# Token stage of a hash-attention and MLP-mixer kernel: the second token weight's sums first on VectorE, the channel weight's sums as two jobs, a fourth place for the last part

## The chip, the cores and the metric

One core of one Trainium2 chip runs the whole kernel. The metric is the device time in microseconds (us) of that core; the kernel before takes 766.55 us, the median of 3 runs (766.54 to 766.57).

## The reference, cut to what matters

```python
# attention: B, H, S, D = 4, 8, 768, 64; only keys in the query's hash bucket count
scores = where(mask, scale * q @ k.T, -1e9); attn = softmax(scores)
x = (attn @ v) as (B, S, H * D)                  # (4, 768, 512)
# token mixing, w_tok1 (768, 256), w_tok2 (256, 768)
xt = x.transpose(0, 2, 1)
h = np.maximum(xt @ w_tok1, 0.0) @ w_tok2
u = x + h.transpose(0, 2, 1)
# channel mixing, w_ch1 (512, 1536), w_ch2 (1536, 512)
h2 = np.maximum(u @ w_ch1, 0.0) @ w_ch2
return u + h2
```

## The kernel before, in words

The program has three stages that follow one another: attention (function `attention`), token mixing (`tokens`), channel mixing (`channels`). Each engine works through its own list of instructions in order; semaphores hold an instruction until what it needs is there. The order of the lists is the order in which the code is written, and the memory of a tile that is given back may be taken by a later tile, whose first write then waits for everything that used the old one.

**The activations.** `XT` in SBUF holds x, later u, transposed: 128 partitions by 4 column blocks by 4 x 768 rows. A copy of x lies in DRAM (`bounced`), from which `tokens` fetches the rows of batch element b into `x0` (b even) or `x1` (b odd).

**The token stage** goes over b = 0 to 3. `mix1(b)` makes the hidden layer in two halves j (24 matmul instructions each, L1226), and ScalarE applies the ReLU after each half (L1233). `left_sums(b)` makes four sums on VectorE (L1249 to L1252). `mix2(b, m)`, m = 0 and 1, makes two column blocks of the second product with seven half-size products in place of eight (L1266), for which it needs sums of the weight `W2`: `weight_sums()` inside `tokens` (L1203 to L1206). Its results go from four PSUM banks by four ScalarE copies (L1271, L1274, L1276, L1278) and five VectorE adds (L1281 to L1285) into a *place* in SBUF, and from there GpSimd's queue starts a transfer that adds the place to `XT` (L1286). There are three places, the three thirds of the later tile `SW2`; part (b, m) takes place (2b + m + 1) mod 3, so part (3,1) takes the place that (2,0) took, and its first copy must wait until the transfer of (2,0) has read it. The eight transfers of GpSimd's queue signal the semaphores DMASW0 to DMASW7 in turn, part (3,1) the last.

**The jobs.** Between the parts, work for the channel stage is done as a list of jobs: one after each half of `mix1`, one between the two parts of `mix2` of b = 0, 1, 2: eleven turns. The first job makes the sums of the channel weight `WC1` (four VectorE operations of 128 x 1536, L1316 to L1321: `early` the first two, `late` the other two), the other eight convert pieces of the second channel weight from 64-bit floats: one operation on ScalarE (L177), then five on VectorE (L187 to L206), 768 columns each.

**The channel stage** begins with the pass `hidden(0, t)`, t = 0 to 5, called row t here. Each row is seven products of 1.72 us (L1353) into four banks, in two pairs of banks; the pairs alternate between two rows. The products 1 to 4 fill the four banks; ScalarE copies three of them (L1359: p1 from the first bank, p5, p7); products 5 to 7 go on adding to banks 1, 3 and 4, each behind the copy of its bank; then a VectorE add makes the first result `R[0]` (L1393), and ScalarE makes a fourth copy, u, of the first bank. Three more adds (L1402) and a bounded difference (L1368) end the row. Between them VectorE makes sums of weights for later (L1858 to L1861 for each part, L1316 to L1321 once more for the second channel weight, on tiles that include the three places), which SyncE's queue stores in DRAM. GpSimd adds two copies per row (L1397). `R[0]` lies in memory that `x0` had.

Of the kernel before, what the change touches and what calls it, by code (L numbers as in the profile page):

```python
# [48 lines left out]
def kernel(  # L49
# [18 lines left out]
    B, NP, _, _, S = qk.shape  # L68
# [1116 lines left out]
    def tokens(pool, psum, W1, W2, x0, weights, jobs, T, places):  # L1185

        x1 = pool.tile([P, NR, DM], F32, name="x1", tag="x1", bufs=1)
        R1 = {}
        turned = not jobs
        if not turned:
            fetch(1, x1)
            jobs = jobs(weights(pool))
            bounce(places[2], NREG - 2)
        NQ = DM // 2
        sums = pool.tile([P, 3, HALF], F32, name="W2sums", tag="W2sums", bufs=1)
        b00, b01, b10, b11 = (W2[:, k, HALF * n : HALF * n + HALF] for k in range(2) for n in range(2))  # L1200

        def weight_sums():
            nc.vector.tensor_tensor(sums[:, 0], b01, b00, op=ALU.subtract)  # L1203
            nc.vector.tensor_tensor(sums[:, 1], b11, sums[:, 0], op=ALU.subtract)
            nc.vector.tensor_tensor(b01, b11, b01, op=ALU.subtract)
            nc.vector.tensor_tensor(sums[:, 2], b10, sums[:, 1], op=ALU.subtract)  # L1206

        def job():
            if not turned and jobs:
                jobs.pop(0)()  # L1210

        def bank(name):
            return psum.tile([P, 512], F32, name=name, tag="mm", bufs=4 if turned else 8)

        def banks():
            return psum.tile([P, 2, 512], F32, name="trp", tag="tr", bufs=2)

        def mix1(b):
            x = (x0, x1)[b % 2]
            if b and turned:  # L1220
                turn(b, x, banks)
            r1 = pool.tile([P, NJ, DM], F32, name="r1", tag="r1", bufs=2)
            for j in range(NJ):
                ps = bank("t1")
                for r in range(NR):
                    nc.tensor.matmul(  # L1226
                        ps, W1[:, r, P * j : P * j + P], x[:, r], start=(r == 0), stop=(r == NR - 1),
                    )
                to = r1[:, j]
                if not turned:  # L1230
                    to = to.rearrange("p (c g i) -> p g c i", c=NCB, i=32)
                    ps = ps.rearrange("p (g c i) -> p g c i", c=NCB, i=32)
                nc.scalar.activation(to, ps, ACT.Relu)  # L1233
                job()
            if b % 2:
                new = pool.tile([P, 3, NQ], F32, name="r1s", tag="r1s", bufs=1)
            else:
                new = T[0].rearrange("p k t -> p (k t)")[:, : 3 * NQ].rearrange("p (i c) -> p i c", i=3)
            R1[b] = r1, new
            if not turned and b + 2 < B:  # L1240
                fetch(b + 2, x)

        def left_sums(b):
            r1, new = R1[b]
            a00, a01, a10, a11 = (
                r1[:, k].rearrange("p (m i c) -> p i m c", m=2, i=2)[:, i] for i in range(2) for k in range(2)
            )
            new = new.rearrange("p i (m c) -> p i m c", m=2)
            nc.vector.tensor_tensor(new[:, 1], a00, a10, op=ALU.subtract)  # L1249
            nc.vector.tensor_tensor(a10, a10, a11, op=ALU.add)  # L1250
            nc.vector.tensor_tensor(new[:, 0], a10, a00, op=ALU.subtract)
            nc.vector.tensor_tensor(new[:, 2], a01, new[:, 0], op=ALU.subtract)  # L1252

        def mix2(b, m):

            r1, new = R1[b]
            a00, a01, s1, a11 = (
                r1[:, k, P * (2 * m + i) : P * (2 * m + i) + P] for i in range(2) for k in range(2)
            )
            new = new[:, :, P * m : P * m + P]  # L1260
            ps = [bank("t2")[:, :HALF] for _ in range(4)]
            to = places[(2 * b + m + 1) % 3].rearrange("p (i n t) -> p i n t", i=2, n=2)
            p1, u, p7, p57 = (to[:, i, n] for i in range(2) for n in range(2))

            def product(at, left, right, start=True):
                nc.tensor.matmul(  # L1266
                    ps[at], left, right, start=start, stop=True, skip_group_check=True,
                )

            product(0, a00, b00)  # L1270
            nc.scalar.copy(p1, ps[0])  # L1271
            product(1, a01, b10)
            product(2, s1, sums[:, 0])
            nc.scalar.copy(p57, ps[2])  # L1274
            product(3, new[:, 1], b01)
            nc.scalar.copy(p7, ps[3])  # L1276
            product(0, new[:, 0], sums[:, 1], False)
            nc.scalar.copy(u, ps[0])  # L1278
            product(2, new[:, 2], b11, False)
            product(3, a11, sums[:, 2], False)  # L1280
            nc.vector.tensor_tensor(p1, ps[1], p1, op=ALU.add)  # L1281
            nc.vector.tensor_tensor(p57, p7, p57, op=ALU.add)
            nc.vector.tensor_tensor(p57, p57, u, op=ALU.add)
            nc.vector.tensor_tensor(p7, ps[3], u, op=ALU.add)
            nc.vector.tensor_tensor(u, ps[2], u, op=ALU.add)  # L1285
            nc.gpsimd.dma_start(  # L1286
                out=XT[:, 2 * m : 2 * m + 2, S * b : S * b + S], in_=to.rearrange("p i n t -> p i (n t)"),
                accum_op=ALU.add,
            )

        for b in range(B):
            mix1(b)
            if b == 0:
                weight_sums()
            left_sums(b)
            if b:
                mix2(b - 1, 0)
                job()
                mix2(b - 1, 1)
        mix2(B - 1, 0)  # L1300
        inputs(0, T, 0)
        mix2(B - 1, 1)
        while not turned and jobs:
            job()

    def weight_sums(w, sums, first, second, low, high):

        a00, a01 = w[:, first, low], w[:, second, low]
        a10, a11 = w[:, first, high], w[:, second, high]

        def early():
            nc.vector.tensor_tensor(sums[:, 1], a00, a10, op=ALU.subtract)  # L1316
            nc.vector.tensor_tensor(a10, a10, a11, op=ALU.add)

        def late():
            nc.vector.tensor_tensor(sums[:, 0], a10, a00, op=ALU.subtract)  # L1320
            nc.vector.tensor_tensor(sums[:, 2], a01, sums[:, 0], op=ALU.subtract)  # L1321

        return [early, late]
# [892 lines left out]
    def inside(stage, *args):  # L2216
        with tc.tile_pool(name="sb", bufs=2, reuse_waits="tile") as pool, tc.tile_pool(
            name="ps", bufs=2, space=PSUM, reuse_waits="tile"
        ) as psum, tc.manual_schedule():
            stage(pool, psum, *args)  # L2220
# [8 lines left out]
    late = ctx.enter_context(ExitStack())  # L2229
    big = {}  # L2230
    n = NHT // 4 * P
# [10 lines left out]
    def attention_and_tokens(W1, W2, x0):  # L2242
        inside(attention, W1, W2, x0)
        pool = late.enter_context(tc.tile_pool(name="late", bufs=1, side="right", reuse_waits="tile"))
        SW1 = big["SW1"] = pool.tile([P, 3, NCB // 2, DCH // 2], F32, name="SW1")
        TA = big["TA"] = pool.tile([P, 2, NCB // 2, TT], F32, name="TA")
        n = NHT * DM

        def second_tile(i):
            return pool.tile([P, (n, n * 3 // 4)[i]], F32, name=f"second{i}", tag=f"second{i}", bufs=1)  # L2250

        WC2 = second["WC2"] = second_tile(0).rearrange("p (k c) -> p k c", k=NHT)
        second["SW2"] = second_tile(1).rearrange("p (i k c) -> p i k c", i=3, k=NHT // 2)
        second["tile"] = second_tile

        def weights(pool):
            return Conversion(pool, [(w_ch2, WC2, 3, (0, NHT))], bufs=3)

        def jobs(conversion):
            early, late = weight_sums(  # L2260
                WC1, SW1, slice(0, NCB // 2), slice(NCB // 2, NCB), slice(0, DCH // 2), slice(DCH // 2, DCH),
            )
            return [
                lambda: (early(), late()),
                *[conversion.one] * (NHT * DM // NW),
            ]

        SW2 = second["SW2"].rearrange("p i k c -> p i (k c)")
        places = [SW2[:, i] for i in range(3)]
        inside(tokens, W1, W2, x0, weights, jobs, [TA[:, 0], None, TA[:, 1], None], places)  # L2270
# [100 lines left out]
```

## Time and profile before

| what | value |
|---|---|
| median of 3 runs | 766.55 us |
| the profiled execution's own time | 767.96 us |
| its span, first to last instruction | 766.2 us |
| TensorE busy (PE) | 758.5 us, 99% of the span |
| VectorE busy (DVE) | 673.5 us, 88% |
| ScalarE busy (ACT) | 442.4 us, 58% |
| token stage, first matmul of `mix1(0)` to the first of row 0 | 289.12 to 367.64 us |
| first channel pass, rows 0 to 5 | 367.64 to 439.74 us |

Durations and starts are read from one profiled execution, in us from the start of its span. A line of the timeline gives the start, the duration, the engine, the line of the kernel, the operation, output<-input, the shape, and in brackets how long the engine stood idle before it and what released it. PEld is TensorE's loading of weights, which runs beside its matmuls; POOL is GpSimd, SP is SyncE's queue of transfers. The 1.76 us by which the execution's time is longer than its span lie outside the instructions.

### The profile page before, as it was taken

To read this page: it belongs to the slowest core of one execution; us is meant where nothing else is said; L and a number is where in the kernel's file an instruction comes from. 1 tells how busy PE (TensorE), PEld (TensorE's weight loads), DVE (VectorE), ACT (ScalarE), POOL (GpSimd) and SP (SyncE) were. 2 spreads that over 40 slices of the span, in tenths; PEclk is the share of its full clock that TensorE was granted. 3 is DMA by queue.
4 is the path that set the end of the run, shared out by engine and by line. 5 is a ranking of instruction groups with operands and counts; after the bars stand their busy time and mean duration, and the time that the engine had idled before them with its cause. 6 is when DMAs were issued, how large, how long until landed. Compare 5 with 4: busy or idle time off the path is not lost.

```text
span 766.2 us, 14575 instructions
## 1 busy us (share of the span) xinstructions
PE 758.5 (99%) x5549; PEld 509.8 (67%) x5549; DVE 673.5 (88%) x969; ACT 442.4 (58%) x816; POOL 189.7 (25%) x266
## 2 busy tenths in 40 slices
PE   9999999999999999999999999999999999999997
PEld 4565655666656554455444468888877888886886
DVE  5899899899997998999788798998899799889884
ACT  6677777677776873333232326566666667665331
POOL 2346771638761820011220100100000011000001
PEclk9999999999999999999999999999999999999999
DMA  7746587575965549876697997889576696750665
GB/s 257 271 172 184 179 240 225 181 179 186 217 202 116 168 68 254 310 178 119 112 321 244 348 360 263 244 233 277 171 220 210 234 261 140 235 157 8 207 157 130
DMA packets 131210, 157.80 MB, mean 206 GB/s; under 512 B 56000, under 2 KB 99520, under 8 KB 129216
## 3 DMA queue, kind: packets, MB, share of 16 engines
q1 hardware_dynamic: 119248, 136.05, 56.3%
q0 software_dynamic: 11600, 20.53, 13.1%
q8 instruction: 45, 0.74, 0.4%
q10 hardware_dynamic: 288, 0.25, 0.1%
q14 instruction: 29, 0.24, 0.1%
HBM read 107.71 MB, written 40.67 MB: 194 GB/s over the span
## 4 chain that ended last, share of the span: by engine, by line
PE 88%; DVE 8%; DMA 2%; issue 1%; SPq 0%; DVEq 0%; ACT 0%; ACTq 0%
PE b L1353 51%; PE sc L503 16%; PE acc L470 14%; PE sc L425 1%; PE hash L536 1%; PE ss L848 1%; DVE size L196 1%; PE sacc L874 1%; DVE unit L195 1%; DMA XT<-second 1%; DVE second L206 1%; PE hash L348 1%; DVE size L191 1%; PE ssums L862 1%; PE hash L353 1%
## 5 line engine op out<-in xcount | busy, mean ns | idle before, releaser
L414 ACT ACTIVATE exps<-sc 128x768 f32<-128x768 f32 (+1 forms) x181 | 126.5, 765 | 10.1 <-PE sc L503 7.2
L1353 PE MATMUL b<-R,second 128*128 128x256 f32 (+1 forms) x522 | 131.8, 408 | 0.0
L503 PE MATMUL sc<-qk 32*128 32x384 f32 (+1 forms) x1352 | 120.1, 457 | 0.0
L1353 PEld LDWEIGHTS b<-R,second 128*128 128x128 f32 x522 | 99.1, 190 | 28.5 <-issue 16.5
L470 PE MATMUL acc<-exps,vn 128*32 128x385 f32 (+1 forms) x1344 | 111.7, 486 | 0.0
L503 PEld LDWEIGHTS sc<-qk 32*128 32x128 f32 x1352 | 92.3, 185 | 16.9 <-issue 4.4
L1359 ACT COPY c<-b 128x256 f32<-128x256 f32 (+1 forms) x96 | 40.3, 426 | 79.3 <-PE b L1353 66.1
L470 PEld LDWEIGHTS acc<-exps,vn 128*32 128x32 f32 x1344 | 43.9, 109 | 62.0 <-issue 60.0
L376 POOL DMA_DIRECT2D bits<-XT x104 | 54.6, 526 | 72.1 <-DVE XT L366 27.4
L459 DVE TENSOR_TENSOR esd<-esd,exps 128x768 f32<-128x768 f32 x70 | 67.0, 957 | 4.3
L1353 PE MATMUL b<-XT,WC 128*128 128x256 f32 (+1 forms) x208 | 61.0, 428 | 0.0
L791 POOL DMA_INDIRECT table<-XT,sorting x48 | 57.1, 1190 | 14.7 <-issue 13.2
L2063 POOL DMA_DIRECT2D out<-second x7 | 8.5, 1213 | 187.3 <-DVE second L2057 81.5
L557 ACT COPY rec<-rec 32x384 f32<-32x384 f32 x56 | 28.5, 510 | 41.0 <-DVE rec L551 39.6
L1353 PEld LDWEIGHTS b<-XT,WC 128*128 128x128 f32 x208 | 39.5, 190 | 15.4 <-issue 10.3
L503 PE MATMUL sc<-bits 32*128 32x384 bf16 (+1 forms) x338 | 48.0, 311 | 0.0
L1353 PE MATMUL b<-XT,SW 128*128 128x256 f32 (+1 forms) x164 | 47.0, 410 | 0.0
L455 DVE TENSOR_TENSOR esd<-esd,exps 128x768 f32<-128x768 f32 x42 | 40.3, 958 | 4.4
L1226 PE MATMUL t<-x,W 128*128 128x512 f32 x96 | 42.1, 594 | 0.2 <-DMA x<-bounced 0.2
L1353 PEld LDWEIGHTS b<-XT,SW 128*128 128x128 f32 x164 | 31.1, 190 | 9.4 <-issue 4.1
L1286 POOL DMA_DIRECT2D XT<-second x8 | 9.9, 1233 | 95.8 <-DVE unit L187 56.2
L1226 PEld LDWEIGHTS t<-x,W 128*128 128x128 f32 x96 | 18.1, 190 | 23.3 <-issue 21.7
(333 smaller groups left out, 1455.9 us busy)
## 6 DMA issues: line engine op xcount, KB each, us to landing
second<-left SPq DMA_DIRECT2D x20, 768.0 KB
qk<-in_qk_rows SPq DMA_DIRECT2D x13, 1152.0 KB
raw<-in_moe_w_ch SPq DMA_DIRECT2D x16, 768.0 KB
second<-left SPq DMA_DIRECT2D x18, 576.0 KB
WC<-hidden_left SPq DMA_DIRECT2D x18, 448.0 KB
x<-bounced SPq DMA_DIRECT2D x4, 1536.0 KB
XT<-second POOLq DMA_DIRECT2D x8, 768.0 KB
seen<-in_qk SPq DMA_DIRECT2D x15, 384.0 KB
```

What stands on the lines that cost most here:

```text
L376: nc.gpsimd.dma_start(out=to[at : at + 2 * BITS, half[j]], in_=g[of : of + 2 * BITS])
L414: return nc.scalar.activation(e[:, :, columns], sc, ACT.Exp, scale=SCALE)
L455: nc.vector.tensor_tensor(self.d, self.d, e, op=ALU.add)
L459: nc.vector.tensor_tensor(self.d, self.d, e, op=ALU.add)
L470: made = nc.tensor.matmul(acc[D * i + d : D * i + d + 32], vn[:, i, c, d : d + 32], e[:, i], start=(c == 0), stop=(c == NR - 1),)
L503: nc.tensor.matmul(made[j, piece][:, i], k[at : at + 32, ks], q[at : at + 32], start=part < 0, stop=part == 1,)
L557: nc.scalar.copy(rec[other : other + 32, h], rec[at : at + 32, h])
L791: nc.gpsimd.indirect_dma_start(out=tables[2 * w + i], out_offset=bass.IndirectOffsetOnAxis(ap=self.at[:, x : x + 1], axis=0), in_=row, in_ ...
L1226: nc.tensor.matmul(ps, W1[:, r, P * j : P * j + P], x[:, r], start=(r == 0), stop=(r == NR - 1),)
L1286: nc.gpsimd.dma_start(out=XT[:, 2 * m : 2 * m + 2, S * b : S * b + S], in_=to.rearrange("p i n t -> p i (n t)"), accum_op=ALU.add,)
L1353: nc.tensor.matmul(ps, left(k), right(k), start=start and k == ks[0], stop=stop and k == ks[-1], skip_group_check=True,)
L1359: nc.scalar.copy(c, ps)
```

## The change

Three edits, all in the token stage:

1. `weight_sums()` of `tokens` is called ahead of the loop over b, no longer after `mix1(0)`.
2. The sums of the channel weight, one job with four VectorE operations, become two jobs with two each. There are now ten jobs in the same eleven turns, so each conversion comes one turn later.
3. Part (3,1) of `mix2`, the last, puts its results into the memory of `x0`, in place of the place that (2,0) used. `x0` holds batch element 2 before, which `mix1(2)` has read.

```diff
-            to = places[(2 * b + m + 1) % 3].rearrange("p (i n t) -> p i n t", i=2, n=2)
+            place = places[(2 * b + m + 1) % 3]
+            if b + 1 == B and m:
+                place = x0.rearrange("p r c -> p (r c)")[:, : 2 * S]
+            to = place.rearrange("p (i n t) -> p i n t", i=2, n=2)
...
+        weight_sums()
         for b in range(B):
             mix1(b)
-            if b == 0:
-                weight_sums()
             left_sums(b)
...
             return [
-                lambda: (early(), late()),
+                early, late,
                 *[conversion.one] * (NHT * DM // NW),
             ]
```

In the changed kernel the lines behind the first edit are numbered 3 higher, those behind the second 2 higher (L1271 becomes L1274, L1393 becomes L1395).

The list of VectorE at the start of the token stage, before. `SW` and `WC` are the channel weight and its sums, `W` is `W2`, `W2sums` its sums, the rows of `unit`, `size` and `second` one conversion:

```order
L1316 TENSOR_TENSOR SW_3789<-WC_85 128x1536
L1317 TENSOR_TENSOR WC_85<-WC_85 128x2x768
L1320 TENSOR_TENSOR SW_3789<-WC_85 128x1536
L1321 TENSOR_TENSOR SW_3789<-WC_85,SW_3789 128x1536
L187 TENSOR_SCALAR unit<-size 128x768
L191 TENSOR_SCALAR size<-size 128x768
L195 SCALAR_TENSOR_TENSOR unit<-raw,unit 128x768
L196 TENSOR_TENSOR size<-size,unit 128x768
L206 SCALAR_TENSOR_TENSOR second_3791<-raw,size 128x3x256
L1203 TENSOR_TENSOR W2sums<-W_109 128x384
L1204 TENSOR_TENSOR W2sums<-W_109,W2sums 128x384
L1205 TENSOR_TENSOR W_109<-W_109 128x384
```

The same place in the changed kernel; the last four rows are `left_sums(0)`:

```order
L1203 TENSOR_TENSOR W2sums<-W_109 128x384
L1204 TENSOR_TENSOR W2sums<-W_109,W2sums 128x384
L1205 TENSOR_TENSOR W_109<-W_109 128x384
L1206 TENSOR_TENSOR W2sums<-W_109,W2sums 128x384
L1318 TENSOR_TENSOR SW_3789<-WC_85 128x1536
L1319 TENSOR_TENSOR WC_85<-WC_85 128x2x768
L1322 TENSOR_TENSOR SW_3789<-WC_85 128x1536
L1323 TENSOR_TENSOR SW_3789<-WC_85,SW_3789 128x1536
L1249 TENSOR_TENSOR TA<-r_3818 128x256
L1250 TENSOR_TENSOR r_3818<-r_3818 128x2x128
L1251 TENSOR_TENSOR TA<-r_3818 128x256
L1252 TENSOR_TENSOR TA<-r_3818,TA 128x256
```

One conversion has moved from ahead of `left_sums(0)` to behind it; from there on, up to `mix2(1,1)`, each step of VectorE has one conversion fewer ahead of it.

The list of ScalarE at `mix1(3)` and the start of `mix2(2,0)`, before:

```order
L1233 ACTIVATE r_4040<-t_4041 128x4x4x32
L177 ACTIVATE size<-raw 128x768
L1233 ACTIVATE r_4040<-t_4057 128x4x4x32
L1271 COPY second_3792<-t_4070 128x384
L1274 COPY second_3792<-t_4072 128x384
L1276 COPY second_3792<-t_4073 128x384
```

And in the changed kernel:

```order
L1233 ACTIVATE r_4032<-t_4033 128x4x4x32
L177 ACTIVATE size<-raw 128x768
L1233 ACTIVATE r_4032<-t_4049 128x4x4x32
L177 ACTIVATE size<-raw 128x768
L1274 COPY second_3792<-t_4070 128x384
L1277 COPY second_3792<-t_4072 128x384
```

The last conversion now begins behind the ReLU of the second half of `mix1(3)`, where it began behind the first half.

The list of VectorE where the token stage ends and row 0 begins, with the semaphores that each row waits for, before:

```order
L1284 TENSOR_TENSOR second_3792<-t_4138,second_3792 128x384 [waits PE_49]
L1181 TENSOR_TENSOR TB<-XT,TA 128x1024
L1285 TENSOR_TENSOR second_3792<-t_4137,second_3792 128x384 [waits DVE_49]
L1183 TENSOR_TENSOR TB<-XT,TB 128x1024 [waits DVE_49]
L1393 TENSOR_TENSOR R_4169<-b_4176,c 128x2x256 [waits DMAHW5_49,PE_49,Activation_49]
L1394 TENSOR_SCALAR R_4169<-R_4169 128x2x256 [waits DVE_49]
```

And in the changed kernel, where `x` is `x0`:

```order
L1287 TENSOR_TENSOR x_110<-t_4138,x_110 128x384 [waits PE_49]
L1288 TENSOR_TENSOR x_110<-t_4137,x_110 128x384 [waits DVE_49]
L1181 TENSOR_TENSOR TB<-XT,TA 128x1024
L1183 TENSOR_TENSOR TB<-XT,TB 128x1024 [waits DVE_49]
L1395 TENSOR_TENSOR R_4169<-b_4176,c 128x2x256 [waits DMASW7_49,PE_49,Activation_49]
L1396 TENSOR_SCALAR R_4169<-R_4169 128x2x256 [waits DVE_49]
```

The first write of `R[0]` waited for the transfer that had fetched batch element 2 into `x0` (DMAHW5); it now waits for DMASW7, the transfer of part (3,1), which reads its place in `x0`.

## The prediction

> **What bounds the kernel now.** First the table of windows: one line per `mix2` part of interest, then the first channel pass and the rest.
>
> ```profile
> core 0: us, PE busy (x) PEld busy (x) DVE busy (x) ACT busy (x) POOL busy (x), PEclk, DMA share, GB/s
> 310.31:314.82 4.51, 4.51 (x15) 2.61 (x14) 4.34 (x9) 3.20 (x6) 0.00 (x0) 1.00 1.04 401
> 314.82:319.60 4.78, 4.78 (x16) 2.58 (x15) 4.64 (x7) 2.54 (x5) 0.00 (x0) 1.00 0.48 157
> 362.77:367.64 4.87, 4.78 (x15) 2.58 (x14) 4.53 (x7) 1.72 (x4) 1.22 (x1) 1.00 0.50 89
> 367.64:439.74 72.10, 72.10 (x169) 31.90 (x168) 56.48 (x85) 18.71 (x34) 11.43 (x8) 1.00 0.85 265
> ```
>
> TensorE sets the end: in the first channel pass it is busy for 72.10 of 72.10 us, at a granted clock of 1.00, so what it loses at any point from here on is lost at the end. In the token stage an undisturbed part takes 4.51 us; part (0,1) takes 4.78 and part (3,1) 4.87. These 0.27 + 0.36 = 0.63 us are all that the three edits can take away there. The timeline shows what held the two parts:
>
> ```profile
> 316.21 0.93 ACT L177 ACTIVATE size<-raw 128x768 f32<-128x768 f32 x1 [2.00 <-DVE second L206]
> 317.03 0.47 ACT L1271 COPY second<-t 128x384 f32<-128x384 f32 x1
> 317.56 0.30 PEld L1266 LDWEIGHTS t<-W2sums,TA 128*128 128x128 f32 x2 [0.61 <-ACT second L1271]
> ...
> 358.57 1.20 POOL L1286 DMA_DIRECT2D XT<-second  x1 [6.89 <-DVE second L1285]
> 365.07 0.48 ACT L1271 COPY second<-t 128x384 f32<-128x384 f32 x1 [2.91 <-DMA XT<-second]
> 365.30 1.22 POOL L1286 DMA_DIRECT2D XT<-second  x1 [5.53 <-issue]
> 365.60 0.91 PE L1266 MATMUL t<-W2sums,r1s 128*128 128x384 f32 x2
> 366.35 0.81 PE L1266 MATMUL t<-W,r1s 128*128 128x384 f32 x2
> 372.05 1.20 POOL L1286 DMA_DIRECT2D XT<-second  x1 [5.53 <-DVE TB L1183]
> 378.80 1.21 POOL L1286 DMA_DIRECT2D XT<-second  x1 [5.55 <-DVE seen L1859]
> ```
>
> At 316.21 a conversion on ScalarE waits for VectorE, which is behind, and the copy of part (0,1) stands behind the conversion. At 365.07 the first copy of part (3,1) waits until the transfer of (2,0), issued at 358.57, has left the place: 6.50 us. And GpSimd's last four transfers go one behind the other, 6.73, 6.75 and 6.75 us apart, though their data are ready long before. The last, part (3,1), is issued at 378.80, inside the channel pass; by the same 6.50 us it lands at 385.30. Nothing in this kernel waits for that: the place is used again in the second channel weight's sums, well after it.
>
> **The change part by part.** *Weight sums first, and one conversion later.* VectorE's total work stays as it is. At (0,1) it has one conversion fewer behind it, so the size tile is free when ScalarE asks, and the 0.27 us go. Of the moved steps, the sums of `W2` are ready earlier than before and run beside `mix1(0)`; the sums of `WC1` end a little later and are needed only in the channel pass. On SyncE's queue the fetch of batch element 2 passes one piece of weight; neither was waited for. These edits I cost at nothing.
>
> The price is at the other end. The last conversion now begins behind the second ReLU of `mix1(3)`:
>
> ```profile
> 344.34 0.60 ACT L1233 ACTIVATE r<-t 128x512 f32<-128x512 f32 x1 [6.02 <-PE t L1226]
> 344.83 0.91 ACT L177 ACTIVATE size<-raw 128x768 f32<-128x768 f32 x1
> 349.43 0.60 ACT L1233 ACTIVATE r<-t 128x512 f32<-128x512 f32 x1 [3.69 <-PE t L1226]
> 349.72 0.55 DVE L187 TENSOR_SCALAR unit<-size 128x768 uint32<-128x768 uint32 x1
> 357.60 0.56 DVE L1285 TENSOR_TENSOR second<-t,second 128x384 f32<-128x384 f32 x1
> ```
>
> That ReLU starts at 349.43 - 0.27 = 349.16; L177 follows 0.49 later (344.34 to 344.83) and takes 0.91: VectorE gets the last conversion at 350.56, not 349.72. From there to the end of the adds of (2,0) it takes 357.60 + 0.56 - 349.72 = 8.44 us, so these end at 359.00, 0.84 later than the 358.16 of before. TensorE does not feel it: `left_sums(3)`, of which
>
> ```profile
> 355.07 0.42 DVE L1252 TENSOR_TENSOR r1s<-r,r1s 128x256 f32<-128x256 f32 x1
> 358.26 0.49 PE L1266 MATMUL t<-W,r 128*128 128x384 f32 x1
> ```
>
> are the last operation and the first matmul of part (3,0), which reads what these sums make, keeps 358.26 - 355.49 = 2.77 us of cover, less the 0.84 and the 0.27. But the chain of transfers feels it: issue 0.41 later (358.57 - 358.16), three spacings of together 20.23, and 6.50 to land: 359.00 + 0.41 + 20.23 + 6.50 = 386.14 for part (3,1). If VectorE should make up the 0.84, it is 385.30.
>
> *The fourth place.* It takes away the wait at 365.07, so 0.36 us go. But `R[0]` lies in the memory of `x0`, and the change makes a transfer the last user of `x0`: the first add of row 0 (L1393, now L1395) waits for part (3,1) to land. What stands around that add:
>
> ```profile
> 376.48 0.69 DVE L1393 TENSOR_TENSOR R<-b,c 128x512 f32<-128x512 f32 x1 [5.29 <-ACT c L1359]
> 377.21 0.59 ACT L1359 COPY c<-b 128x512 f32<-128x512 f32 x1 [1.43 <-DVE R L1393]
> 378.60 0.56 DVE L1860 TENSOR_TENSOR seen<-seen,SW 128x384 f32<-128x384 f32 x1
> 379.20 2.53 DVE L1861 TENSOR_TENSOR seen<-SW,seen 128x384 f32<-128x384 f32 x1
> 379.54 1.76 POOL L1397 TENSOR_TENSOR c<-c 128x512 f32<-128x512 f32 x1
> 383.29 0.58 ACT L1359 COPY c<-b 128x512 f32<-128x512 f32 x1 [5.50 <-PE b L1353]
> 384.05 1.75 DVE L1316 TENSOR_TENSOR second<-second 128x1536 f32<-128x1536 f32 x1
> 386.52 1.88 PE L1353 MATMUL b<-TB,SW 128*128 128x512 f32 x4
> 389.41 2.71 DVE L1321 TENSOR_TENSOR second<-second,second 128x1536 f32<-128x1536 f32 x1
> 392.04 0.68 DVE L1393 TENSOR_TENSOR R<-b,c 128x512 f32<-128x512 f32 x1
> 392.75 0.58 ACT L1359 COPY c<-b 128x512 f32<-128x512 f32 x1 [3.91 <-DVE R L1393]
> 398.54 1.88 PE L1353 MATMUL b<-TB,SW 128*128 128x512 f32 x4
> 403.15 0.68 DVE L1393 TENSOR_TENSOR R<-b,c 128x512 f32<-128x512 f32 x1
> 410.56 1.88 PE L1353 MATMUL b<-TB,SW 128*128 128x512 f32 x4
> ```
>
> Without the new wait L1395 would start at 376.48 - 0.63 = 375.85; with it, at 386.14, 10.29 us late. Queued behind it on VectorE is everything of rows 0 and 1. Queued behind it on ScalarE, and this is what counts: copy u of each row waits for this add (377.21 and 392.75, released by L1393), and behind u in ScalarE's list stands copy p1 of the next row, without which product 5 of that row (L1353 at 386.52) may not start.
>
> Row 1: u starts 0.73 after the add starts (377.21 - 376.48), at 386.87, takes 0.59, p1 takes 0.58 and ends at 388.04; product 5 starts 0.05 behind. Its time without the wait is 386.52 - 0.63 = 385.89. TensorE loses 2.2 us, and some 0.1 for starting again (0.91 for the two matmuls at 365.60, 0.81 at 366.35): 2.3.
>
> Row 2: from the add of row 0 to that of row 1 (392.04 - 376.48 = 15.56 us, second weight sums included) VectorE had hardly a gap:
>
> ```profile
> 376.48:392.04 15.56, 15.56 (x37) 6.84 (x36) 15.35 (x14) 3.29 (x6) 5.13 (x3) 1.00 0.87 247
> ```
>
>  In it L1861 took 2.53 us beside a GpSimd add, where the like row before took 0.56. In the changed kernel that GpSimd add, which waits for ScalarE alone, runs while VectorE stands still, so I take 15.56 - 1.97 = 13.59: the add of row 1 starts at 399.73, u at 400.46, p1 ends at 401.63, product 5 at 401.68. Its time without would be 398.54 - 0.63 + 2.3 = 400.21: 1.5 lost, 0.1 for starting again, 1.6.
>
> The Trainium skill ("SBUF — State Buffer", section "Who interferes with whom") says that a VectorE instruction with two SBUF inputs and a GpSimd instruction that reads SBUF hold a common port in turn, the later fully blocked. By that rule the 1.97 us go with the overlap, as taken; were the stretch of another origin and stayed, the sum would be 1.97 us higher.
>
> Row 3: 399.73 + (403.15 - 392.04) = 410.84 for the add of row 2, 0.73 + 0.59 + 0.58 more to the end of p1: 412.74, against 410.56 - 0.63 + 3.9 = 413.83. Nothing more is lost: 1.1 us of cover.
>
> Sum: -0.63 + 2.3 + 1.6 = +3.3 us. Nothing behind gives it back, since TensorE has no gap in the pass. The profiled execution takes 767.96 us (span 766.2) and would take 771.3; the runs without a profile have a median of 766.55, 1.41 lower, and I add the 3.3 to that: 769.8.
>
> Bounds: the row 2 condition fixes the sum, so a transfer landing 0.84 earlier (385.30) gives 2.4, one landing 1 later (a slower transfer than the 6.50) 4.3. VectorE's stretch: if also the 2.71 - 1.75 = 0.96 that L1321 spends beside GpSimd goes (L1316, the same size, takes 1.75 at 384.05), 2.3; if nothing goes, 5.3. Both low: 1.5, or 768.0. Both high: 6.3, or 772.8.
>
> **The rivals.** *The transfer is early.* The last adds of part (3,1) and the size of its transfer:
>
> ```profile
> 369.50 0.55 DVE L1285 TENSOR_TENSOR second<-t,second 128x384 f32<-128x384 f32 x1
> ```
>
> ```profile
> XT<-second POOLq DMA_DIRECT2D x8, 768.0 KB
> ```
>
> If GpSimd's transfers did not run one behind the other, part (3,1) would be issued 0.41 after these adds, at 370.46, and land 6.50 later at 376.96, 1.1 us behind 375.85. Copy p1 of row 1 is not due until 383.29, so that is hidden; the two gains stay, 765.9. Against it speak three nearly equal spacings, and GpSimd's idle 5.5 us before each issue while data were ready. It decides if the landing comes some 3.9 us (the 2.3 and 1.6) ahead of 386.14, by 382.3. The Trainium skill ("DMA: Bandwidth & Descriptors", section "Anatomy of one DMA — SWDGE (gpsimd) path") puts such a transfer at 2.0 us plus its bytes at 436 GB/s; an estimate from that page for 768 KB is 3.8 us. By that rule the chain would be over before row 0's add and this rival holds; the trace has 6.50 and 6.7 for it, and the measurement decides.
>
> *TensorE does not feel the wait.* If only the banks tied TensorE to VectorE, not ScalarE's order, row 2 would need row 0's add and nothing would stall: 765.9. Against: the two releases of u by L1393. For: at 383.29 p1 waited for TensorE alone, so no row shows yet how a late u holds p1 up.
>
> *The lateness lasts.* In row 2 the add starts 410.84 - (401.68 + 1.88) = 7.3 us behind the end of product 5; before it was 403.15 - (398.54 + 1.88) = 2.7. VectorE is 4.6 us further behind TensorE. In the pass it is busy 56.48 of 72.10 us, so it should make that up by row 5; but in
>
> ```profile
> 440.00:475.00 35.00, 35.00 (x140) 26.34 (x139) 32.40 (x47) 15.91 (x36) 0.61 (x1) 1.00 0.85 306
> ```
>
> it is busy 32.40 of 35.00, and what remains of the lateness there would stall the first products of the output stage. If 3 of the 4.6 us remain, they come on top: 769.8 + 3 = 772.8. GpSimd's adds, which meet a busy VectorE in each row (up to 1.97 us, as at 379.20), speak for it.
>
> **How the numbers follow.** Forecast 769.8: 0.75, since each link is a row of the trace. Lateness lasts: 0.12. Transfer early: 0.08. TensorE does not feel it: 0.05. A measurement here tells 0.2% from no change, 1.5 us. Both early cases (0.13) give -0.63, no change; the rest is slower, but for a sliver at 768.0; faster is left at 0.01. The range reaches from 767.9, the low bounds, to 772.7, nearly the high ones; outside it lie the 0.13 and about 0.06 of the lasting case.
>
> **What would show it.** Right: part (3,1) takes 4.51 us; part (0,1) too; L1395 of row 0 starts near 386, released by the transfer of `XT` from `x0`; ScalarE's u behind it; TensorE's product 5 of rows 1 and 2 late by about 2.3 and 1.6 us, no stall in row 3. Wrong: L1395 near 376, or near 386 with rows 1 and 2 unhurt; a landing away from 386.1; a gap of TensorE past row 5.

## The result, and the profile after

The changed kernel takes 770.72 us, the median of 4 runs (770.08 to 772.09), against 766.55 in the same job: 1.0057 times as long, 95% interval 1.0039 to 1.0074. A second job gave 771.13 against 767.28: 1.0053, interval 1.0039 to 1.0067. The ratio is not exactly that of the two medians: by the medians the change costs 4.17 and 3.85 us, by the ratios 4.4 and 4.1. So it costs some 3.9 to 4.4 us; 3.3 were forecast, and the 769.8 lie 0.9 under the measurement.

The table of windows for the first trace of the changed kernel: parts (0,1) and (3,1) of the token stage, then rows 0, 1 and 2 of the first channel pass, then the whole pass.

```profile
core 0: us, PE busy (x) PEld busy (x) DVE busy (x) ACT busy (x) POOL busy (x), PEclk, DMA share, GB/s
313.46:317.97 4.51, 4.51 (x15) 2.66 (x14) 4.27 (x9) 2.19 (x5) 0.00 (x0) 1.00 0.99 364
361.15:365.66 4.51, 4.51 (x15) 2.66 (x14) 4.37 (x8) 1.92 (x4) 0.86 (x1) 1.00 0.64 114
365.66:377.68 12.02, 12.02 (x30) 5.32 (x28) 4.38 (x6) 1.66 (x3) 1.55 (x2) 1.00 0.74 131
377.68:393.64 15.96, 13.98 (x30) 5.83 (x28) 8.67 (x12) 3.31 (x6) 4.05 (x3) 0.89 0.58 161
393.64:405.66 12.02, 12.02 (x30) 5.25 (x29) 10.86 (x14) 3.41 (x6) 1.69 (x1) 1.00 0.88 313
365.66:441.71 76.05, 74.07 (x170) 32.35 (x169) 53.90 (x86) 18.96 (x34) 11.38 (x9) 0.98 0.80 245
```

Both parts are down to 4.51 us. The pass has gone from 72.10 to 76.05, and all of it lies in row 1: 15.96 in place of 12.02. The timeline of the same trace, around the new wait:

```profile
358.01 1.20 POOL L1289 DMA_DIRECT2D XT<-second  x1 [11.31 <-DVE second L1288]
361.99 0.48 ACT L1274 COPY x<-t 128x384 f32<-128x384 f32 x1 [1.46 <-PE t L1269]
378.28 1.21 POOL L1289 DMA_DIRECT2D XT<-x  x1 [5.51 <-PE b L1355]
384.84 0.69 DVE L1395 TENSOR_TENSOR R<-b,c 128x512 f32<-128x512 f32 x1 [14.62 <-PE b L1355]
385.56 2.05 ACT L1361 COPY c<-b 128x512 f32<-128x512 f32 x4 [11.76 <-DVE R L1395]
386.69 2.50 PE L1355 MATMUL b<-TB,SW 128*128 128x512 f32 x4 [1.98 <-ACT c L1361]
388.98 3.10 PE L1355 MATMUL b<-XT,SW 128*128 128x512 f32 x4
```

Part (3,1)'s first copy (361.99) waits for TensorE alone; its transfer, the one out of `x`, is issued at 378.28, and 6.56 us later the first add of row 0 starts. (The bracket of that add names TensorE in this trace; in the experiments below it names the transfer.) ScalarE's copies come at once behind it (u first, p1 second of the four in the row at 385.56), and product 5 of row 1 after a gap of 1.98. Then comes what was not forecast: products 5 and 6, 1.88 us each as a rule, take 2.50 and 3.10. The granted clock in steps of half a microsecond tells why:

```profile
387.70:388.20 0.50, 0.50 (x3) 0.21 (x2) 0.50 (x2) 0.00 (x0) 0.50 (x1) 0.82 0.00 0
388.20:388.70 0.50, 0.50 (x2) 0.27 (x1) 0.50 (x1) 0.00 (x0) 0.50 (x1) 0.50 0.00 0
...
391.20:391.70 0.50, 0.50 (x2) 0.19 (x1) 0.50 (x2) 0.44 (x1) 0.00 (x0) 0.77 1.05 378
391.70:392.20 0.50, 0.50 (x2) 0.19 (x1) 0.50 (x1) 0.00 (x0) 0.00 (x0) 1.00 1.03 363
```

From about 388.0 to 391.4 (the shares 0.82 and 0.77 place the two edges) TensorE had half its clock: 3.4 us, of which half is lost, 1.7. Row 1's excess of 3.94 is about the forecast 2.3 and these 1.7. Row 2, by contrast, has no gap, where 1.6 was forecast. Whether one has to do with the other was the first question for the experiments.

### The profile page after: what moved, and what is told of

The parts are those of the page before. It is cut to its first block, busy times and chain, and to the rows that moved or that the text cites. A ratio compares the mean times of both kernels' runs of the same rounds, so it can differ in the third digit from the quotient of the medians.

```text
span 768.4 us, 14577 instructions
## 1 busy us (share of the span) xinstructions
PE 758.3 (99%) x5549; PEld 506.2 (66%) x5549; DVE 670.8 (87%) x969; ACT 443.4 (58%) x816; POOL 191.3 (25%) x266
## 4 chain that ended last, share of the span: by engine, by line
PE 91%; DVE 4%; DMA 2%; issue 1%; POOL 1%; ACT 0%; SPq 0%; DVEq 0%; ACTq 0%; POOLq 0%
PE b L1355 49%; PE sc L503 14%; PE acc L470 12%; PE t L1269 5%; PE t L1226 4%; PE hash L536 1%; DMA x<-bounced 1%; PE sc L425 1%; PE ss L848 1%; PE sacc L874 1%; DMA hidden_left<-second 1%; PE ssums L862 1%; PE hash L348 1%; POOL bits L376 1%; PE hash L353 0%
## 5 line engine op out<-in xcount | busy, mean ns | idle before, releaser
L503 PEld LDWEIGHTS sc<-qk 32*128 32x128 f32 x1352 | 90.5, 185 | 19.6 <-issue 5.9
## 6 DMA issues: line engine op xcount, KB each, us to landing
second<-left SPq DMA_DIRECT2D x20, 768.0 KB
raw<-in_moe_w_ch SPq DMA_DIRECT2D x16, 768.0 KB
```

Source lines behind the costliest of these rows:

```text
L503: nc.tensor.matmul(made[j, piece][:, i], k[at : at + 32, ks], q[at : at + 32], start=part < 0, stop=part == 1,)
```

## The experiments

The theory is that of the prediction: the loss comes from row 0's first add, which waits for GpSimd's *last* transfer, and it reaches TensorE through ScalarE's order. The rival at this point: it comes from the two reorderings, or from any use of `x0` as a place.

**The place for part (2,0).** All three edits, but `x0` goes to the first of the four late transfers:

```diff
-            if b + 1 == B and m:
+            if b + 2 == B and not m:
                 place = x0.rearrange("p r c -> p (r c)")[:, : 2 * S]
```

> All three edits, but the fourth place goes to part (2,0), the first of GpSimd's last four transfers, and part (3,1) takes the place that (2,0) had (its last user before is part (0,1), long landed). Theory (the loss is the wait of row 0's first add for the LAST transfer): the add now waits for a transfer issued at 358.01 in the changed kernel, landing 6.5 later near 364.5, some 9 us ahead of the 374 at which the add can start; so the add starts near 374, no gap of TensorE in rows 1 and 2, granted clock 1.00 throughout the pass, parts (0,1) and (3,1) at 4.51: 766.55 - 0.63 = 765.9, at most 765.7 by the 0.77 that the token stage has gained in the changed kernel's trace. Rival 1 (it is the two reorderings, or any GpSimd transfer out of x0, that costs): the loss of some 4 us stays, 769.9 to 770.7. Rival 2 (the transfer of (3,1), out of the old place, is late for the second channel weight's sums, which write that place): the last of those sums begins 389.4 before, the landing is near 386, so no more than a few tenths: 766.2.

Measured: 766.07 against 766.64, ratio 0.9994, interval 0.9985 to 1.0003, so not yet to be told from before. It was timed once more:

> The version with the fourth place for part (2,0) once more, for a closer time. Theory: the token stage is 0.62 us shorter than before, the rest is as before, so the median lies 0.5 to 0.7 under that of the kernel before in the same job, and the channel pass takes 72.10 at clock 1.00 again. Rival (the 0.6 are within what executions differ by, and something else costs as much): same median within 0.2.

Measured: 766.50 against 767.28, ratio 0.9988, interval 0.9980 to 0.9997: faster than before by 0.8 us by the medians, 0.6 in the first job. Its windows, from the first matmul of `mix1(1)` to row 0, then the pass:

```profile
299.66:366.78 67.12, 67.12 (x184) 35.07 (x185) 64.07 (x99) 25.59 (x47) 6.91 (x6) 1.00 0.78 202
366.78:438.88 72.10, 72.10 (x169) 31.90 (x168) 54.75 (x87) 18.72 (x34) 11.58 (x9) 1.00 0.86 266
```

and the same two stretches of the kernel before:

```profile
299.90:367.64 67.74, 67.65 (x184) 34.85 (x185) 64.70 (x103) 25.30 (x47) 7.46 (x6) 1.00 0.78 203
```

(Its pass is the 72.10 shown in the prediction.) The reorderings and a place in `x0` give 67.74 - 67.12 = 0.62, and cost nothing in the pass; the rival falls.

**The place alone.** The kernel before with the third edit only, against the changed kernel:

```diff
-        weight_sums()
         for b in range(B):
             mix1(b)
+            if b == 0:
+                weight_sums()
...
-                early, late,
+                lambda: (early(), late()),
```

> The kernel before with the third edit alone: part (3,1) puts its results into x0. Theory: the last transfer is issued at 378.80 as before and lands at 385.30, and row 0's first add starts then, not 10 us earlier; product 5 of row 1 may start at 385.30 + 0.73 + 0.59 + 0.58 = 387.20 against 386.52 - 0.36 = 386.16: a gap of 1.0, 0.1 for starting again. If the granted clock stays at 1.00 after so short a gap, row 2 loses 1.5 more: -0.36 + 1.1 + 1.5 = +2.3, 768.8. If the clock halves after the gap as in the changed kernel (1.7 lost), row 2 loses nothing: -0.36 + 1.1 + 1.7 = +2.4, 769.0. Rival (the loss comes from the reorderings, the place only gives its 0.36): 766.2.

Measured: 769.62 against 766.64, ratio 1.0040, interval 1.0027 to 1.0053; 769.0 or 768.8 were expected. Rows 1 and 2 in its windows, and product 5 of each in its timeline (lines behind the edit are numbered one higher than in the changed kernel):

```profile
377.88:390.94 13.06, 12.28 (x30) 5.23 (x28) 7.00 (x11) 3.31 (x6) 3.40 (x3) 1.00 0.57 149
390.94:404.63 13.69, 12.28 (x29) 5.24 (x28) 13.48 (x15) 3.31 (x6) 1.54 (x1) 1.00 0.90 319
```

```profile
383.83 0.69 DVE L1396 TENSOR_TENSOR R<-b,c 128x512 f32<-128x512 f32 x1 [13.83 <-DMA XT<-x]
385.69 1.98 PE L1356 MATMUL b<-TB,SW 128*128 128x512 f32 x4 [0.78 <-ACT c L1362]
399.38 1.98 PE L1356 MATMUL b<-TB,SW 128*128 128x512 f32 x4 [1.41 <-ACT c L1362]
```

Here the clock stayed at 1.00, and row 2 has its gap: 1.04 lost in row 1 (expected 1.1) and 1.67 in row 2 (expected 1.5). The releaser of the add is now named as the transfer. The loss belongs to the third edit.

**The reorderings alone.** The first two edits without the fourth place:

```diff
-            if b + 1 == B and m:
-                place = x0.rearrange("p r c -> p (r c)")[:, : 2 * S]
```

> The first two edits without the fourth place. Theory: part (0,1) gains its 0.27; but the chain of GpSimd's transfers starts later by what the last conversion loses (issue 359.22 against 358.57, when the 1.21 us by which the changed kernel's token stage starts earlier are put back), so the transfer of (2,0) lands 0.65 later and the first copy of part (3,1), which waits for it, holds TensorE up by 0.65 + 0.27 = 0.92 more: -0.27 + 0.92 = +0.65, 767.2. Row 0's first add waits for nothing new and starts near 376. Rival (the wait at part (3,1) has cover that the trace of before doesn't show): only the gain is left, 766.3. Rival 2 (the reorderings are what costs 4 us): 770.

Measured: 767.23 against 766.64, ratio 1.0009, interval 1.0001 to 1.0018: +0.6, as the theory has it. Part (3,1)'s first copy in its timeline (its L1272 is L1274 of the changed kernel):

```profile
364.62 0.48 ACT L1272 COPY second<-t 128x384 f32<-128x384 f32 x1 [4.00 <-DMA XT<-second]
365.15 0.91 PE L1267 MATMUL t<-W2sums,r1s 128*128 128x384 f32 x2 [1.17 <-ACT second L1272]
```

The wait for the old place, 2.91 before, is 4.00, since the chain of transfers begins later; TensorE loses 1.17 there. So the reorderings by themselves are a loss, and the fourth place is what makes them worth having.

**A landing one transfer earlier.** All three edits, with `x0` for part (3,0), the last but one (part (3,1) takes the place that part (1,1) used):

```diff
-            place = places[(2 * b + m + 1) % 3]
-            if b + 1 == B and m:
+            place = places[1 if b + 1 == B else (2 * b + m + 1) % 3]
+            if b + 1 == B and not m:
```

> All three edits, but the fourth place goes to part (3,0), the last but one of the four transfers; part (3,1) takes the place that part (1,1) used. Row 0's first add then waits for a landing one spacing (6.7) earlier than in the changed kernel: issue 371.57 + 6.56 = 378.1 in its trace, some 4 us behind the 374 at which the add could start. Theory (a late add costs TensorE nothing until it is later than copy p1 of row 1 can bear): u is done near 379.5, p1 is due near 381.5, so no gap in row 1; VectorE stands 4 us behind and makes it up, row 2 has no gap; clock 1.00; the pass takes 72.1 and the time is that of the version with (2,0) in x0, 0.12% under before. Rival (each us by which VectorE is late reaches the output stage): up to 4 us more, 0.4% over before.

Measured: 766.57 against 766.68, ratio 0.9999, interval 0.9990 to 1.0009. The interval excludes the rival's 4 us (0.4% over); the expected 0.12% (0.9988) lies just below it, and no gain is shown by the times. The trace is clearer. Row 0's add, copy u behind it and p1 of row 1, then the pass:

```profile
378.10 0.69 DVE L1395 TENSOR_TENSOR R<-b,c 128x512 f32<-128x512 f32 x1 [7.98 <-PE b L1355]
378.83 0.59 ACT L1361 COPY c<-b 128x512 f32<-128x512 f32 x1 [4.87 <-DVE R L1395]
381.47 0.59 ACT L1361 COPY c<-b 128x512 f32<-128x512 f32 x1 [2.05 <-PE b L1355]
```

```profile
365.82:437.92 72.10, 72.10 (x170) 31.90 (x169) 55.79 (x86) 18.73 (x34) 11.62 (x9) 1.00 0.86 266
```

The add starts 12.28 us behind the start of row 0, where it started 8.84 behind it before (376.48 and 367.64): 3.4 late. Copy u still waits for it, but p1 waits for TensorE as it did before, and the pass is the 72.10 of before; from `mix1(1)` to row 0 it takes 67.13, so that it has the gain of the version with (2,0) in `x0`. A late add is free until u is later than p1's due time.

**Copy u behind p1.** The changed kernel with its wait, but in rows 0 and 1 ScalarE makes u after p1 and p5 of the next row:

```diff
+            if tails:
+                tails.pop()()
             p7 = copy(ps[3], c[2])
...
-            u = copy(ps[0], c[3])
-            for k, a in [(3, p7), (1, ps[2]), (2, ps[3])]:
-                nc.vector.tensor_tensor(r[k], split(a), split(u), op=ALU.add)
+            def tail():
+                u = copy(ps[0], c[3])
+                for k, a in [(3, p7), (1, ps[2]), (2, ps[3])]:
+                    nc.vector.tensor_tensor(r[k], split(a), split(u), op=ALU.add)
...
+                for job in jobs.pop(0) if jobs else []:
+                    job()
...
+            tails.append(tail)
+            if t > 1:
+                tails.pop()()
```

> The changed kernel, wait and all, but in rows 0 and 1 ScalarE makes copy u (with the VectorE additions behind it) after copies p1 and p5 of the NEXT row, so that a late add no longer holds p1 up. Theory (the wait reaches TensorE only through ScalarE's order): row 0's add still starts near 385, released by the transfer, but product 5 of row 1 starts on time and the clock stays at 1.00; the third copy p7 of row 2 stands behind the late u of row 1 and may cost some 0.5, row 3 some 0.1, the output stage the 0.2 of the changed kernel: 766.55 - 0.77 + 0.8 = 766.6. Rival (VectorE's lateness reaches TensorE by the banks as well): gaps in rows 1 to 3 of 2 us and more stay, 769 or more.

Measured: 774.43 against 766.64, ratio 1.0097, interval 1.0082 to 1.0112: worse than the changed kernel. The time that I expected is refuted; the measured one is in the rival's range (769 or more), but the rival's gaps of 2 us and more in rows 1 to 3 are not there. The timeline of row 1:

```profile
385.86 1.88 PE L1355 MATMUL b<-TB,SW 128*128 128x512 f32 x4
386.06 0.59 ACT L1361 COPY c<-b 128x512 f32<-128x512 f32 x1 [2.85 <-PE b L1355]
386.92 1.07 ACT L1361 COPY c<-b 128x512 f32<-128x512 f32 x2 [0.28 <-DVE R L1398]
388.05 1.13 PE L1355 MATMUL b<-XT,SW 128*128 128x512 f32 x2 [0.31 <-ACT c L1361]
```

Product 5 does start without a gap, with the add as late as in the changed kernel (at 386.19, 19.21 behind the start of row 0; 385.22 - 366.01 is 19.21 in the third trace of the changed kernel, below), so that link of the theory stands: it was ScalarE's order. But product 6 starts 0.06 behind the end of the *second* copy of the pair at 386.92, p7, and not behind p5, which began at 386.06 and took 0.59 (the first of the pair is u); why product 6 waits for p7 too is not shown. p7 now stands behind u, and the gap has only moved by a product. TensorE lost 0.57 in row 1 and 1.56 in row 2 (12.59 and 13.58 us), less than the changed kernel, and then waited 0.3, 0.5 and 2.8 us for VectorE in the output stage. Why that stage suffers so much more here is not settled; the same edit also moved the weight sums and their stores.

**Which way the loss is made up.** The changed kernel once more, unaltered, for three more traces.

> The changed kernel once more, unaltered, to see how its loss is made up in another execution. Theory: the gap of TensorE in row 1, about 2.0 us, is there in each execution; what follows it varies. Either the granted clock halves behind it for some 3.5 us as in the first trace (1.75 lost) and row 2 then waits for nothing, the pass taking 76.0 us; or the clock stays at 1.00 and row 2 has the forecast gap of 1.6, the pass taking 72.1 + 2.1 + 1.6 = 75.8. Both give about the same time, median 770 to 771. Rival (the halved clock is not tied to the gap but to the stretch of the program): it shows at the same place whether there is a gap or not, and row 2 never has a gap.

> The changed kernel once more for a profile. Two executions so far had the granted clock at 0.50 for some 3.5 us behind the gap in row 1 and no gap in row 2; of its ten runs five have a mean clock of 1.00. Theory: where the clock stays at 1.00, row 2 has the forecast gap of about 1.6 us, and the pass takes 75.8 against 76.05. Rival: no gap in row 2 in that case either, so that the pass takes 74.2.

> The same again: pass 76.05 us with the clock halved behind the gap, or 75.8 with the clock at 1.00 and a gap of 1.6 in row 2 (theory), or 74.2 with neither (rival).

Measured: 771.13 (median of 6), 771.09 and 771.61 (one each). The second trace is like the first: gap of 1.99, halved clock, no gap in row 2. The third and the fourth are of the other kind. The third, rows 1, 2 and the pass, then the adds and product 5 of the two rows, and a wait in the output stage:

```profile
378.02:392.32 14.30, 12.28 (x29) 5.24 (x28) 7.00 (x11) 3.32 (x6) 4.04 (x3) 1.00 0.52 136
392.32:406.02 13.70, 12.29 (x29) 5.24 (x28) 13.49 (x15) 3.31 (x6) 1.54 (x1) 1.00 0.90 319
366.01:442.07 76.06, 72.63 (x169) 31.75 (x168) 54.91 (x86) 18.86 (x34) 11.24 (x9) 1.00 0.80 244
```

```profile
385.22 0.69 DVE L1395 TENSOR_TENSOR R<-b,c 128x512 f32<-128x512 f32 x1 [14.64 <-DMA XT<-x]
387.07 1.98 PE L1355 MATMUL b<-TB,SW 128*128 128x512 f32 x4 [2.02 <-ACT c L1361]
388.41 1.75 DVE L1404 TENSOR_TENSOR R<-c 128x512 f32<-128x512 f32 x1
398.93 0.68 DVE L1395 TENSOR_TENSOR R<-b,c 128x512 f32<-128x512 f32 x1
400.77 1.98 PE L1355 MATMUL b<-TB,SW 128*128 128x512 f32 x4 [1.41 <-ACT c L1361]
438.20 0.32 SPq L1879 DMA_DIRECT2D hidden_left<-seen  x1
438.91 0.69 DVE L1395 TENSOR_TENSOR R<-b,c 128x512 f32<-128x512 f32 x1 [2.03 <-PE b L1355]
445.74 0.56 DVE L1860 TENSOR_TENSOR seen<-WC 128x384 f32<-128x384 f32 x1 [1.10 <-DMA hidden_left<-seen]
459.61 4.12 PE L1355 MATMUL b<-R,second 128*128 128x256 f32 x18 [0.60 <-DVE R L2008]
```

With the clock at 1.00 row 1 loses 2.28 and row 2 loses 1.68, as forecast, so the rivals by which row 2 never has a gap fall; with the clock halved row 1 loses 3.94 and row 2 nothing, because TensorE is then late enough itself for what VectorE brings. The pass takes 76.05 or 76.06 in either case: the two losses stand for each other and don't add up. That both are about 1.7 us is a coincidence: one is half of 3.4 us of half clock, the other what VectorE's stretch of row 2 asks for.

**Is it the gap that halves the clock?** The kernel before with copy p1 made several times over in rows 1 to 5, so that product 5 waits for ScalarE:

```diff
             p1 = copy(ps[0], c[0])
+            for _ in range(9 if t else 0):
+                copy(ps[0], c[0])
```

> The kernel before with ScalarE's copy p1 made ten times over in rows 1 to 5 (into the same tile, nothing else changed). p1 ends 2.65 us before product 5 is due, and a copy behind a copy takes 0.51, so nine more hold product 5 up by 4.6 - 2.65 = 1.95 and TensorE has a gap like the changed kernel's in each of five rows. Theory (it is a gap of about 2 us that halves the granted clock, in some cases and not in others): in one to four of the five rows the clock falls to 0.50 within 2 us behind the gap and stays there for about 3.5, 1.75 lost each; the pass takes 72.1 + 5 x 2.05 = 82.4 plus 1.75 for each. Rival (the halved clock in the changed kernel had another cause than the gap): clock 1.00 in all five rows, 82.4.

> The same with twelve more copies: gaps of 6.1 - 2.65 = 3.5 us in rows 1 to 5. Theory: a gap of this length halves the clock in all or nearly all of the five rows, each for about 3.5 us, so the pass takes 72.1 + 5 x 3.6 + 5 x 1.75 = 98.9. Rival (the gap is not what halves it): 90.1 at clock 1.00.

Measured: 790.37 and 803.94. A copy behind a copy took 0.62, not 0.51, so the gaps are 2.79 and 4.64. Rows 1, 2 and 5 with nine copies (rows 3 and 4 take 16.77 at 0.90 like row 1), and rows 1 and 2 with twelve:

```profile
380.12:396.89 16.77, 13.98 (x29) 5.83 (x28) 15.17 (x16) 8.46 (x15) 3.42 (x3) 0.90 0.99 308
396.89:411.97 15.08, 12.29 (x30) 5.24 (x28) 7.09 (x13) 8.46 (x15) 1.27 (x1) 1.00 0.56 189
445.51:462.29 16.78, 13.99 (x30) 5.83 (x28) 9.97 (x19) 8.46 (x15) 1.83 (x2) 0.90 0.70 258
```

```profile
380.18:399.79 19.61, 14.97 (x29) 6.26 (x28) 15.21 (x16) 10.21 (x18) 2.94 (x3) 0.83 0.86 268
399.79:418.14 18.35, 13.71 (x30) 5.83 (x28) 7.09 (x13) 10.21 (x18) 1.27 (x1) 0.91 0.45 150
```

Four of five rows lose 16.77 - 15.08 = 1.69 us more than the fifth, whose clock stayed at 1.00: the same gap, two outcomes. With gaps of 4.64 the clock falls in all five rows (0.82 to 0.91). The gap is the cause.

Why one of 2 to 3 us has the effect at one time and not at another, the traces show too: the clock changes in steps. With nine copies it falls at 391.32, 422.04, 439.10 and 456.17, which lie 9, 5 and 5 times 3.413 us apart, and each time it is back one such step later; with twelve copies it is back after one step or two. Counted in these steps from the edges of its own clock, each trace can be cut up, and what matters is how long TensorE works within the step. Four steps, the one ahead of the fall in the first trace of the changed kernel, the ones with the gaps of rows 1 and 2 with nine copies, and the one with the 2.8 us in the output stage of the version with u behind p1:

```profile
384.60:388.02 3.42, 1.44 (x4) 0.68 (x4) 3.08 (x6) 2.05 (x4) 0.33 (x1) 1.00 0.00 0
387.90:391.32 3.42, 1.38 (x3) 0.68 (x4) 3.35 (x3) 3.33 (x8) 0.38 (x1) 1.00 1.03 372
404.97:408.38 3.41, 1.67 (x4) 0.87 (x5) 0.00 (x0) 3.35 (x7) 0.66 (x1) 1.00 0.84 260
460.26:463.67 3.41, 1.45 (x7) 1.32 (x8) 3.38 (x5) 0.00 (x0) 0.00 (x0) 1.00 0.98 396
```

The clock fell at the end of the first two steps and not of the other two. In these 13 traces, while matmuls run, it falls 11 times, each time behind a step with at most 1.44 us of matmuls; no other step at full clock holds less than 1.45. That border is read from these traces alone, and it rests on one step just above it. So, as far as these traces go, the place of the gap in the steps decides: in the third trace of the changed kernel a border at 385.95 (112 steps ahead of that clock's next edge, at 768.24) splits the 2.02 us into 0.90 and 1.12, and the clock stays. Where the steps begin differs from one execution to the next, so a gap of 2 us still has two prices.

## Why the prediction was right, and what it missed

**The gains.** Forecast 0.27 + 0.36; both parts take 4.51, and 0.62 is what the version with (2,0) in `x0` shows from `mix1(1)` to row 0. Right.

**The chain of transfers.** Forecast: landing at 386.14 with row 0 at 367.01. The first trace has row 0 at 365.66, 1.35 earlier, and the add at 384.84; put back by 1.35 that is 386.19. Right to 0.05. The transfer took 6.56; the estimate by the Trainium skill ("DMA: Bandwidth & Descriptors", section "Anatomy of one DMA — SWDGE (gpsimd) path"), 3.8, and the rival of an early transfer fall.

**Row 1.** Forecast 2.3; 2.28 where the clock held. The step had no term for the clock: where it halved, the row lost 3.94.

**Row 2.** Forecast 1.6 by a stretch of VectorE of 13.59 from add to add; measured 1.68 and 13.71 (385.22 to 398.93) where the clock held, and no loss where it halved. The operation that took 2.53 beside GpSimd is down to 0.56, as taken. That the stretch came out right is luck beyond that, by two differences that nearly cancel: L1321's 2.71, which I had kept, is down as well (its successor L1323 takes 1.76), 0.95 less; but GpSimd's add of row 1 now runs from 388.07 to 389.61, beside the first of L1404 (388.41), which takes 1.75 in place of about 0.68, 1.07 more. The rule of the Trainium skill on the shared port ("SBUF — State Buffer", section "Who interferes with whom") agrees with these rows: the overlap goes from one pair of instructions and comes back at another.

**Row 3** loses nothing (406.02 to 418.04 in the third trace, 12.02). Right.

**Nothing behind gives it back, and the lateness doesn't last.** This is the step that failed, in its second half. VectorE does make up its lateness by row 5, as argued: row 5's add waits 2.03 for TensorE (438.91), 2.10 before. But the stores of the weight sums on SyncE's queue don't. A store of `seen` is issued at 438.20, 72.19 behind the start of row 0; before, it was

```profile
434.50 0.32 SPq L1877 DMA_DIRECT2D hidden_left<-seen  x1
442.17 0.55 DVE L1858 TENSOR_TENSOR seen<-WC 128x384 f32<-128x384 f32 x1
```

66.86 behind it, 5.33 less, of which the pass's own 3.96 is only a part: the store is 1.37 late against TensorE. VectorE's next write of `seen`, which stood in line without a wait before, waits 1.10 for it, and TensorE waits 0.60 for VectorE at 459.61. In the first trace the three are smaller together: the store 0.95 late, a wait of 0.74, then one of 0.2 of TensorE. That the one brings about the other is read from this order; no run took the store's wait away. From the end of the pass to the end of the span the third trace takes 769.4 - 442.07 = 327.33, before 766.2 - 439.74 = 326.46: +0.87, of which 0.60 is this wait. The version with the place alone has the same: 768.0 - 440.69 = 327.31 from the end of its pass. The rival named the output stage and VectorE, at 3 us; it was the output stage by way of the store queue, at 0.9.

The sum as it now stands, for a trace with the clock at 1.00: -0.61 (67.13 from `mix1(1)` to row 0, against 67.74) + 2.28 + 1.68 + 0.87 = +4.22, against +3.3 forecast and 3.9 to 4.4 measured. In the first trace, with the clock halved, the pass adds 3.95 and what follows it 768.4 - 441.71 - 326.46 = 0.23: about +3.6.

**The step from the profile to the runs.** The profiled execution of before was slower than its other runs by 1.41; most of it lies in the attention stage, which ended at 289.12 there and at 287.91 in the first trace of the changed kernel, though nothing in it was changed. Adding a difference to the median, not to that execution's time, was the right way, though by the number alone the 771.3 would have come nearer to 770.72: its 1.41 too many stand for the 0.9 that the sum lacks.

## What to carry to other kernels

When a buffer is lent for a second use, look at who takes its memory next, and give it to the *earliest* of the users that compete: here the change costs 4 us with the spare tile lent to the last transfer of a queue, and gains 0.6 to 0.8 with the same tile lent to the first. A late instruction costs nothing until the first one behind it on any engine is due, so follow the late one through each in-order list, the store queue too: an engine that has caught up can still wait for a store that hasn't. And price a gap of a busy TensorE with a range, not with its length: one of 2 us cost row 1 2.3 or 3.9.

## What the runs showed of the hardware

A gap of TensorE between matmuls can halve its granted clock for a time after. In the token and channel stages gaps of up to 1.42 us never did; of about 2.0 us, in 2 of 4; of 2.79, in 4 of 5; one of 2.82 (the output stage of the version with u behind p1) did not; of 4.64, in 5 of 5. It fell at the end of a step of 3.413 us with at most 1.44 us of matmuls in it, and, while matmuls ran, at no other. In the first trace the clock fell 1.3 us *behind* the end of the gap (at 388.0, the gap ended at 386.69) and stayed at 0.50 for about 3.4 us, so that 1.7 were lost. The Trainium skill ("TensorE: Matmul & The Clock Gate", section "Part 1: The HAM clock gate") tells of a free-running window of about 3.4 us by which the clock is set; the steps of 3.413 us, and the two outcomes of equal gaps, agree with that. It puts the fall behind at least one idle window of that length; here a window with 1.44 us of matmuls was enough, and gaps of 2.0 and 2.79 in six cases, so the measurement decides against a whole idle window.
